# A written order of single operations for the attention part, with the softmax division on ScalarE

## The chip, the core and the metric

The kernel runs on one core of one Trainium2 chip. The core's engines work side by side, each on its own instruction queue in the order in which the queue was written: TensorE multiplies matrices (PE in the profile, PEld for its weight loads), VectorE (DVE) and ScalarE (ACT) work elementwise, GpSimd (POOL) helps in the last part, and SyncE (SP) issues DMA transfers. They hand work to each other through semaphores. The metric is the device time of one execution in microseconds; the median of three runs of the kernel before is 886.98 us (886.62 to 888.88).

## The reference

Three layers follow each other, all in float32. The first is local attention with block summaries, over 2 batches, 8 heads, 768 positions and head dimension 64:

```python
k_sum = k.reshape(B, H, nb, block, D).max(axis=3)        # block 32
v_sum = v.reshape(B, H, nb, block, D).mean(axis=3)
scores_l = where(|i - j| < 16, scale * q @ k.T, -1e9)
scores_s = scale * q @ k_sum.T + log(block)
a = exp(concat(scores_l, scores_s) - max)
a = a / (sum(a) + 1e-9)
x = a @ concat(v, v_sum)                                 # 1536 tokens x 512
```

The second is a PReLU layer, `g = max(h, 0) + alpha * min(h, 0)` with `h = x @ w_in` (512 to 2048), then `g @ w_out`. The third is four experts of width 1024, weighted by normalized probabilities: `out += p[:, e] * (relu(x @ w1[e]) @ w2[e])`. The weights of the second layer arrive as 64-bit words, which the kernel takes apart on the chip.

## The kernel before

**The first part** holds the attention and the first quarter of the PReLU layer, woven into each other. Its order is the table `ORDER`: a list of short names, each of them one step, and the loop at line 625 issues the steps one after the other under a manual schedule. On each engine, and in SyncE's DMA queue, instructions stand in just that order. The first two letters of a name say which step, the digits which piece of the work:

- Attention goes by 24 half-tiles (128 tokens, 4 of the 8 heads). `fa`, `fb` and `fc` load keys, queries and values, `ka` and `va` whole rows of keys and values for the block summaries, `kb` takes the maximum over blocks (line 154) and `vb` the sum (line 164). For half-tile i: `sa` scores on TensorE (line 200), `sb` mask and row maximum on VectorE (line 210), `sc` four exponentials with their row sums on ScalarE (line 219), `na` the division by the sums (lines 224 to 229), `ta` four transposes on TensorE (line 235), `tb` a copy out of PSUM on ScalarE, `xa` probabilities times values on TensorE (line 253), `xb` and `xc` the split of the result into a high and a low half. The tile `sm` of scores, later of probabilities, has three buffers: it is taken by `sb` and given back by `ta`.
- The weights come in pieces of 128 x 512, 16 of them in this part. `wa` loads a piece of 64-bit words (line 282, tile `raw`, three buffers), `wb` cuts out the exponent (line 286), `wc` shifts it on ScalarE (line 291), `wd` builds the fraction (two instructions, lines 296 and 299), `we` the value (three, lines 305 to 309), `wf` the high half on ScalarE (line 314), `wg` the low half (line 320).
- The PReLU layer goes by blocks of 256 tokens. `la` to `le` are a first-layer product of twelve matmuls and its evacuation (the first of them in time is `la01`), `ma` and `mb` a second-layer product and its sum.

**After the table** a scheduler that works from a timeline of its own places the rest of the PReLU layer (matmuls of 512 columns; weight pieces by `w_step`, side by side with the products), and then the 32 expert steps. Both parts run through the same TensorE queue, so the second part begins where the first ends.

Of the kernel before, what the change touches and what calls it, by code (L numbers as in the profile page):

```python
# [8 lines left out]
F32 = mybir.dt.float32  # L9
F32R = mybir.dt.float32r  # L10
U32 = mybir.dt.uint32
AF = mybir.ActivationFunctionType
ALU = mybir.AluOpType
# [4 lines left out]
P = 128  # L18
# [5 lines left out]
NK = KW + NB  # L24
# [22 lines left out]


ORDER = (
# [30 lines left out]
)  # L80
MASK_OFF = -1.0e9 * math.sqrt(D)
EXP_LOW = float((1023 - 127 + 20) << 20)
EXP_TOP = float((255 - 20) << 20)
# [3 lines left out]
def kernel(  # L87
# [15 lines left out]
    nc = tc.nc  # L103
# [10 lines left out]
    att = first.enter_context(tc.tile_pool(name="att", bufs=2))  # L114
# [20 lines left out]
    st = {}  # L135
# [79 lines left out]
    def a_exp(i):  # L215
        sm, mx = st["p", i], st.pop(("m", i))
        st["e", i] = sume = att.tile([P, 4], F32, tag="sume", name="sume", bufs=3)
        for u in range(4):
# [2 lines left out]
                accum_out=sume[:, u:u + 1],  # L221
            )

    def a_norm(i):
        pp, sume = st["p", i], st.pop(("e", i))
        r = att.tile([P, 4, 1], F32, tag="r", name="r")
        nc.vector.tensor_scalar(r[:, :, 0], sume, 1e-9, None, op0=ALU.add)
        nc.vector.reciprocal(r, r)
        nc.vector.tensor_tensor(pp, pp, r.to_broadcast([P, 4, NK]), op=ALU.mult)  # L229

    def a_transpose(i):
        pp = st.pop(("p", i))
# [41 lines left out]
    ws, pw = {}, {}  # L274

    def w_load(p):
        if p >= len(pieces):
            return
        k, i = pieces[p]
        t = wp.tile([P, DM, 2], U32, tag="raw", name="raw", bufs=3)  # L280
        pw[p] = [t]
        return nc.sync.dma_start(out=t.rearrange("p n w -> p (n w)"), in_=wa_in[k, i])

    def w_mask(p):
        e = wp.tile([P, DM], F32, tag="e", name="e")
        nc.vector.tensor_scalar(e.bitcast(U32), pw[p][0][:, :, 1], 0x7FF00000, None, op0=ALU.bitwise_and)
        pw[p].append(e)

    def w_exp(p):
        e = pw[p][1]  # L290
        nc.scalar.activation(e, e.bitcast(U32), AF.Relu, bias=ebias)

    def w_frac(p):
        raw = pw[p][0]
        t = wp.tile([P, DM], F32, tag="t", name="t")
        nc.vector.tensor_scalar(  # L296
            t.bitcast(U32), raw[:, :, 1], 0x000FFFFF, 0x00100000, op0=ALU.bitwise_and, op1=ALU.bitwise_or
        )
        nc.vector.scalar_tensor_tensor(t, raw[:, :, 0], 2.0 ** -32, t.bitcast(U32), op0=ALU.mult, op1=ALU.add)  # L299
        pw[p].append(t)  # L300

    def w_value(p):
        raw, e, t = pw[p]
        eu = e.bitcast(U32)
        nc.vector.tensor_scalar(eu, e, EXP_TOP, 8.0, op0=ALU.min, op1=ALU.mult)  # L305
        nc.vector.scalar_tensor_tensor(  # L306
            eu, raw[:, :, 1], 0x80000000, eu, op0=ALU.bitwise_and, op1=ALU.bitwise_or
        )
        nc.vector.tensor_tensor(t, t, e, op=ALU.mult)  # L309

    def w_high(p):
# [9 lines left out]
        ws[k, i] = ws[k, i], lo  # L321

    def w_step(p):
        for f in (w_mask, w_exp, w_frac, w_value, w_high, w_low):
            f(p)
        w_load(p + 3)

# [278 lines left out]
    def block(f):  # L606
        return lambda u, j: f(j, u * C0, C0)

    def column(f):
# [4 lines left out]
        "va": v_load, "vb": v_sum, "vc": v_rows,  # L614
        "vd": lambda b: v_mean(b, 0), "ve": lambda b: v_mean(b, 1),
        "fa": load_kw, "fb": load_q, "fc": load_vw,
        "sa": a_scores, "sb": a_max, "sc": a_exp, "na": a_norm, "ta": a_transpose, "tb": a_copy,
        "xa": a_pv, "xb": a_xh, "xc": a_xl,
        "wa": w_load, "wb": w_mask, "wc": w_exp, "wd": w_frac, "we": w_value, "wf": w_high, "wg": w_low,
        "la": block(l1_product), "lb": block(l1_minus), "lc": block(l1_prelu), "ld": block(l1_high),  # L620
        "le": block(l1_low), "ma": column(l2a_product), "mb": column(l2a_sum),
    }
# [14 lines left out]
    for p in range(4 * G, 4 * G + 3):  # L637
        w_load(p)
# [9 lines left out]
    for u, (n, c0, size) in enumerate(units):  # L648
        last = u + 1 == len(units)
        main = [lambda j=j: l1_step(u, j) for j in range(1, G)]  # L650
        if not last:
            main.append(lambda: l1_step(u + 1, 0))
        main += l2_steps(u)
        if n < NG1 - 1:
            p0 = (n + 1) * 2 * G
            lo, hi = ((c0 * 2 * G // (B * S)), ((c0 + size) * 2 * G // (B * S)))
            side = [lambda p=p: w_step(p) for p in range(p0 + lo, min(p0 + hi, len(pieces)))]
        elif c0 == 0:
            side = [lambda: e_load_a(0), lambda: e_load_b(0)]
        elif not last:  # L660
            side = e_prep(0)
        else:
            side = sum(x_combine(0, lambda: gp.tile([P, TP], F32, tag="m", name="m", bufs=2)), [])
        merge(main, side)
# [82 lines left out]
```

## Time and profile before

| | |
|---|---|
| median of 3 runs | 886.98 us |
| the profiled execution | 888.12 us, span 886.3 us |
| TensorE (PE) busy | 834.1 us (94%) |
| TensorE weight loads (PEld) | 739.3 us (83%) |
| VectorE (DVE) busy | 561.8 us (63%) |
| ScalarE (ACT) busy | 391.0 us (44%) |
| GpSimd (POOL) busy | 325.3 us (37%) |
| granted TensorE clock, mean | 0.986 |

The span runs from the first to the last instruction. Busy shares are means over a program whose parts have different limits, so the table alone does not say which engine sets the time; windows of time and the order of single instructions do. A line number is that of the kernel before. In a timeline row the first number is the start in us, the second the length; on VectorE and ScalarE an instruction often starts a little before the end of the one in front of it, so what an instruction costs its engine is the distance to the next start.

### The profile page before, as it was taken

How to read it: one execution, taken by the hardware profiler on the slowest of the kernel's cores; microseconds unless marked ns; L12 is line 12 of the kernel's file. 1: busy time of each engine (PE TensorE's matmuls, PEld its weight loads, DVE VectorE, ACT ScalarE, POOL GpSimd, SP SyncE). 2: the span in 40 equal slices, each digit the busy share in tenths (PEclk: the TensorE clock that was granted, in tenths of full speed). 3: DMA queues.
4: the chain of work that ended last, by engine and by line, in shares of the span. 5: the costliest groups of instructions: out<-in, count | busy, mean ns of one | idle time of the engine just before them, and what ended most of it. 6: DMA issues, size and time to landing. Idle time of an engine off the chain costs nothing.

```text
span 886.3 us, 12629 instructions
## 1 busy us (share of the span) xinstructions
PE 834.1 (94%) x4616; PEld 739.3 (83%) x4616; DVE 561.8 (63%) x1167; ACT 391.0 (44%) x891; POOL 325.3 (37%) x326
## 2 busy tenths in 40 slices
PE   2478989999999999999999999999999999999998
PEld 1367888988888888888988999899898999999896
DVE  6998999797786344665554544555855455455544
ACT  3465877553332232463444343444444444344420
POOL 0000000000002230176766667575566666657400
PEclk9789999999999999999999999999999999999999
DMA  9686663131121000021313121121321212112001
GB/s 322 227 242 194 192 181 109 50 118 39 57 72 48 24 24 24 1 72 50 94 48 95 48 90 54 53 91 48 124 91 48 96 47 92 52 63 81 25 1 71
DMA packets 39550, 76.60 MB, mean 86 GB/s; under 512 B 3776, under 2 KB 15296, under 8 KB 39488
## 3 DMA queue, kind: packets, MB, share of 16 engines
q1 hardware_dynamic: 38912, 75.51, 26.7%
q8 instruction: 36, 0.59, 0.3%
q10 hardware_dynamic: 576, 0.28, 0.1%
q14 instruction: 26, 0.21, 0.1%
HBM read 72.63 MB, written 3.15 MB: 85 GB/s over the span
## 4 chain that ended last, share of the span: by engine, by line
PE 82%; DVE 13%; DMA 2%; ACT 1%; issue 1%; ACTq 0%; SPq 0%; DVEq 0%
PE l L394 55%; PE cb L503 15%; PE cd L503 7%; PE ca L503 3%; DVE sm L210 1%; PE s L200 1%; DMA kv<-in_kt 1%; DVE t L299 1%; DVE sm L229 1%; DVE e L306 1%; DVE t L309 1%; DMA vcat<-in_vw 1%; DVE vs L164 1%; DVE e L305 1%; DMA prob_sb<-in_probs 1%
## 5 line engine op out<-in xcount | busy, mean ns | idle before, releaser
L348 POOL TENSOR_TENSOR w0l<-ra,w0h 128x512 fp32r<-128x512 f32 (+1 forms) x64 | 66.2, 1035 | 331.8 <-DVE t L296 263.9
L573 DVE SCALAR_TENSOR_TENSOR acc<-l,prob_sb,acc 128x512 f32<-128x512 f32 x180 | 130.2, 747 | 85.7 <-PE l L394 85.3
L394 PE MATMUL l<-w1h,gh 128*128 128x512 f32 x384 | 150.2, 392 | 1.6 <-ACT gh L519 1.0
L394 PE MATMUL l<-w1l,gh 128*128 128x512 f32 x384 | 150.8, 393 | 0.0
L394 PE MATMUL l<-w1h,gl 128*128 128x512 f32 x384 | 145.3, 394 | 0.0
L348 POOL TENSOR_TENSOR w1l<-rb,w1h 128x512 fp32r<-128x512 f32 x64 | 83.6, 1309 | 120.1 <-ACT w1h L347 120.1
L348 POOL TENSOR_TENSOR w0l<-s,w0h 128x512 fp32r<-128x512 f32 x64 | 83.9, 1311 | 37.3 <-ACT w0h L347 36.8
L394 PE MATMUL l<-xh,w0h 128*128 128x512 f32 (+1 forms) x240 | 85.0, 354 | 3.0 <-DVE gl L426 2.1
L394 PE MATMUL l<-gh,w1h 128*128 128x512 f32 (+1 forms) x240 | 83.8, 352 | 3.0 <-ACT gh L420 2.9
L394 PEld LDWEIGHTS l<-w1h,gl 128*128 128x128 f32 x384 | 71.9, 188 | 15.7 <-DVE gl L520 0.4
L394 PEld LDWEIGHTS l<-w1h,gh 128*128 128x128 f32 x384 | 72.1, 188 | 13.7 <-ACT gh L519 1.4
L394 PE MATMUL l<-gh,w1l 128*128 128x512 f32 (+1 forms) x240 | 83.4, 349 | 0.0
L394 PE MATMUL l<-xl,w0h 128*128 128x512 f32 (+1 forms) x240 | 83.4, 347 | 0.0
L394 PE MATMUL l<-xh,w0l 128*128 128x512 f32 (+1 forms) x240 | 83.2, 347 | 0.0
L394 PE MATMUL l<-gl,w1h 128*128 128x512 f32 (+1 forms) x240 | 81.7, 351 | 1.4 <-DVE gl L426 1.4
L347 ACT ACTIVATE w0h<-s 128x512 fp32r<-128x512 f32 x64 | 40.5, 632 | 94.4 <-PE cd L503 71.8
L394 PEld LDWEIGHTS l<-w1l,gh 128*128 128x128 f32 x384 | 72.1, 188 | 11.0
L347 ACT ACTIVATE w1h<-rb 128x512 fp32r<-128x512 f32 x64 | 40.5, 632 | 77.7 <-PE l L394 56.1
L503 PE MATMUL cb<-xeh,w0h 128*128 128x384 f32 x192 | 64.7, 337 | 0.1
L503 PE MATMUL cb<-xeh,w0l 128*128 128x384 f32 x192 | 64.7, 337 | 0.0
L503 PE MATMUL cb<-xel,w0h 128*128 128x384 f32 x192 | 64.7, 337 | 0.0
L347 ACT ACTIVATE w0h<-ra 128x256 fp32r<-128x256 f32 (+1 forms) x64 | 33.6, 525 | 56.4 <-PE cb L503 36.5
(112 smaller groups left out, 1797.2 us busy)
## 6 DMA issues: line engine op xcount, KB each, us to landing
raw<-in_wa SPq DMA_DIRECT2D x32, 512.0 KB, 4.2
ra<-in_wb SPq DMA_DIRECT2D x64, 256.0 KB, 3.8
rb<-in_wb SPq DMA_DIRECT2D x32, 512.0 KB, 3.6
q<-in_qh SPq DMA_DIRECT2D x24, 256.0 KB, 4.2
kw<-in_kw SPq DMA_DIRECT2D x24, 192.0 KB, 4.7
vcat<-in_vw SPq DMA_DIRECT2D x12, 384.0 KB, 4.4
kv<-in_kt SPq DMA_DIRECT2D x8, 384.0 KB, 4.1
kv<-in_vt SPq DMA_DIRECT2D x8, 384.0 KB, 4.7
```

Of the source, the lines that this page charges most:

```text
L164: nc.vector.tensor_reduce(vs[:, hp, KW:NK], st.pop(("v", b, hp)), axis=AX.X, op=ALU.add)
L200: nc.tensor.matmul(sp[:, u], q[:, u // 2, u % 2], kw[:, :, u // 2, u % 2], start=True, stop=True)
L210: nc.vector.tensor_tensor_reduce(sm[:, u], sp[:, u], mask[:, m], -1.0 / math.sqrt(D), 3.0e38, ALU.add, ALU.min, mx[:, u:u + 1],)
L229: nc.vector.tensor_tensor(pp, pp, r.to_broadcast([P, 4, NK]), op=ALU.mult)
L299: nc.vector.scalar_tensor_tensor(t, raw[:, :, 0], 2.0 ** -32, t.bitcast(U32), op0=ALU.mult, op1=ALU.add)
L305: nc.vector.tensor_scalar(eu, e, EXP_TOP, 8.0, op0=ALU.min, op1=ALU.mult)
L306: nc.vector.scalar_tensor_tensor(eu, raw[:, :, 1], 0x80000000, eu, op0=ALU.bitwise_and, op1=ALU.bitwise_or)
L347: nc.scalar.activation(hi, src, AF.Copy)
L348: nc.gpsimd.tensor_tensor(lo, src, hi.bitcast(F32), op=ALU.subtract)
L394: ins = nc.tensor.matmul(ps, a, c, start=(i == 0), stop=(i == n - 1))
L503: nc.tensor.matmul(ps, l, r, start=(first and i == 0), stop=(i == len(terms) - 1), skip_group_check=True)
L573: nc.vector.scalar_tensor_tensor(acc2[:, t], ps, pe, acc2[:, t], op0=ALU.mult, op1=ALU.add)
```

## The change

Three things change, all in the first part.

1. The division `na` becomes three steps. `na` adds the guard 1e-9 to the sums, `nb` takes the reciprocal, both on VectorE with 128 x 4 elements, and `nc` multiplies the probabilities on ScalarE: four ACTIVATE instructions of 128 x 120 with the reciprocal as a scale per partition, in place of one VectorE multiplication of 128 x 480.
2. The weight steps are cut up: `wd` and `we` are now the two instructions of the fraction, `wf`, `wg` and `wh` the three of the value, `wi` the high half on ScalarE and `wj` the low half. What they compute stays as it was.
3. `ORDER` is written anew, with 694 names in place of 598. All loads, half-tiles, pieces and products are the same; they stand in another order.

```diff
-    "ka00 ka01 fa0 fb0 fc0 wa3 wa1 wa0 fa1 kb00 fb1 fa2 fb2 kb01 va00 fc2 fa3 kc00 va01 sa0 sb0 fb3 "
+    "ka00 fa0 ka01 fb0 kb00 kb01 kc00 fb2 fa2 sa0 sb0 ka03 sc0 sa2 kb03 sb2 wa1 na0 wb1 ka02 fb4 fa1 "
...
+    def a_guard(i):
+        st["r", i] = r = att.tile([P, 4], F32, tag="r", name="r", bufs=3)
+        nc.vector.tensor_scalar(r, st.pop(("e", i)), 1e-9, None, op0=ALU.add)
+
+    def a_recip(i):
+        nc.vector.reciprocal(st["r", i], st["r", i])
+
     def a_norm(i):
-        pp, sume = st["p", i], st.pop(("e", i))
-        r = att.tile([P, 4, 1], F32, tag="r", name="r")
-        nc.vector.tensor_scalar(r[:, :, 0], sume, 1e-9, None, op0=ALU.add)
-        nc.vector.reciprocal(r, r)
-        nc.vector.tensor_tensor(pp, pp, r.to_broadcast([P, 4, NK]), op=ALU.mult)
+        pp, r = st["p", i], st.pop(("r", i))
+        for u in range(4):
+            nc.scalar.activation(pp[:, u], pp[:, u], AF.Copy, scale=r[:, u:u + 1])
...
-        for f in (w_mask, w_exp, w_frac, w_value, w_high, w_low):
+        for f in (w_mask, w_exp, w_mant, w_frac, w_top, w_sign, w_value, w_high, w_low):
```

The next two pieces are VectorE's queue just behind the first half-tile's row maxima. `e` and `t` are the exponent and fraction of a weight piece, `r` the reciprocal sums of a half-tile, `sm` its probabilities; the number tells one buffer from another. Before:

```order
L286 TENSOR_SCALAR e_160<-raw_119 128x512
L296 TENSOR_SCALAR t_162<-raw_119 128x512
L299 SCALAR_TENSOR_TENSOR t_162<-raw_119,t_162 128x512
L227 TENSOR_SCALAR r_166<-sume_155 128x4
L228 RECIPROCAL r_166<-r_166 128x4
L229 TENSOR_TENSOR sm_146<-sm_146,r_166 128x480
L305 TENSOR_SCALAR e_160<-e_160 128x512
L306 SCALAR_TENSOR_TENSOR e_160<-raw_119,e_160 128x512
L309 TENSOR_TENSOR t_162<-t_162,e_160 128x512
L286 TENSOR_SCALAR e_180<-raw_121 128x512
```

Now, in the same place, though behind the maxima of two half-tiles in place of one (the line numbers are the changed kernel's):

```order
L230 TENSOR_SCALAR r_157<-sume_138 128x4
L295 TENSOR_SCALAR e_159<-raw_155 128x512
L305 TENSOR_SCALAR t_167<-raw_155 128x512
L158 TENSOR_REDUCE ksum_95<-kv_161 128x24
L316 TENSOR_SCALAR e_159<-e_159 128x512
L233 RECIPROCAL r_157<-r_157 128x4
L312 SCALAR_TENSOR_TENSOR t_167<-raw_155,t_167 128x512
L320 SCALAR_TENSOR_TENSOR e_159<-raw_155,e_159 128x512
L162 COPY kw10_98<-ksum_95 128x96
L162 COPY kw11_99<-ksum_95 128x96
L326 TENSOR_TENSOR t_167<-t_167,e_159 128x512
L230 TENSOR_SCALAR r_199<-sume_182 128x4
```

The multiplication of `sm` is gone from here, and between an instruction and the one that reads its result there now stands at least one other: the reciprocal, the fraction's second instruction, the sign and the product each have such a neighbour in front of them, where before five of ten rows read what the row above had just written.

The next two pieces are ScalarE's queue at its start. `sm` with `mx` and `sume` are exponentials, `sm` with `r` the new multiplications, `w0h` the high half of a weight piece. Before:

```order
L219 ACTIVATE sm_218,sume_225<-sm_218,mx_219 128x120 x4
L314 ACTIVATE w0h_239<-t_215 128x512
L291 ACTIVATE e_243<-e_243,ebias_87 128x512
L240 ACTIVATE ptb_256<-pt_245 120x512
L291 ACTIVATE e_263<-e_263,ebias_87 128x512
L314 ACTIVATE w1h_275<-t_253 128x512
```

Now:

```order
L223 ACTIVATE sm_130,sume_138<-sm_130,mx_131 128x120 x4
L300 ACTIVATE e_159<-e_159,ebias_87 128x512
L223 ACTIVATE sm_149,sume_182<-sm_149,mx_150 128x120 x4
L238 ACTIVATE sm_130<-sm_130,r_157 128x120 x4
L331 ACTIVATE w0h_203<-t_167 128x512
L300 ACTIVATE e_201<-e_201,ebias_87 128x512
L238 ACTIVATE sm_149<-sm_149,r_199 128x120 x4
```

Each half-tile now stands in ScalarE's queue twice before its transposes, once for the exponentials and once for the multiplications, and the exponentials of the next half-tile stand between the two.

## Rows read from the trace of the kernel before

**Rows 1.** Windows: us, busy time (instructions), TensorE clock, DMA share, GB/s
```profile
0.00:62.00 62.00, 27.37 (x205) 23.61 (x205) 52.14 (x163) 29.98 (x95) 0.74 (x6) 0.84 0.84 270
62.00:181.50 119.50, 108.78 (x1057) 102.97 (x1056) 108.42 (x349) 79.67 (x263) 0.00 (x0) 0.98 0.48 145
88.00:133.00 45.00, 41.16 (x419) 38.72 (x420) 43.77 (x163) 34.92 (x124) 0.00 (x0) 1.00 0.62 188
181.50:370.00 188.50, 188.50 (x833) 156.13 (x832) 120.03 (x207) 67.56 (x115) 23.85 (x24) 1.00 0.14 45
370.00:886.30 516.30, 509.46 (x2527) 456.56 (x2525) 281.17 (x452) 213.84 (x421) 300.71 (x296) 1.00 0.20 66
```
**Rows 2.** Timeline, TensorE: first 256-column product, first of 512 columns
```profile
61.99 0.56 PE L394 MATMUL l<-xh,w0h 128*128 128x256 f32 x1
...
180.95 0.40 PE L394 MATMUL l<-xh,w0h 128*128 128x512 f32 x1
```
**Rows 3.** Waits of VectorE, 10 to 144 us: total, times, longest
```profile
DVE sm L210 <- PE s L200: 2.1, 2, 1.5
```
**Rows 4.** Timeline, VectorE, 106.1 to 111.6 us
```profile
106.10 0.42 DVE L286 TENSOR_SCALAR e<-raw 128x512 uint32<-128x512 uint32 x1
106.43 0.42 DVE L296 TENSOR_SCALAR t<-raw 128x512 uint32<-128x512 uint32 x1
106.89 0.69 DVE L299 SCALAR_TENSOR_TENSOR t<-raw,t 128x512 f32<-128x512 uint32 x1
107.50 0.48 DVE L416 SCALAR_TENSOR_TENSOR l<-m,beta,l 128x256 f32<-128x256 f32 x1
...
108.22 0.16 DVE L227 TENSOR_SCALAR r<-sume 128x4 f32<-128x4 f32 x1
108.42 0.18 DVE L228 RECIPROCAL r<-r 128x4 f32<-128x4 f32 x1
108.63 0.66 DVE L229 TENSOR_TENSOR sm<-sm,r 128x480 f32<-128x480 f32 x1
109.20 0.42 DVE L426 TENSOR_TENSOR gl<-l,gh 128x256 fp32r<-128x256 f32 x1
109.54 0.41 DVE L305 TENSOR_SCALAR e<-e 128x512 uint32<-128x512 f32 x1
109.99 0.69 DVE L306 SCALAR_TENSOR_TENSOR e<-raw,e 128x512 uint32<-128x512 uint32 x1
110.71 0.69 DVE L309 TENSOR_TENSOR t<-t,e 128x512 f32<-128x512 f32 x1
111.32 0.28 DVE L210 CUSTOM_DVE_ANT_0 sm<-s,mask 128x120 f32<-128x120 f32 x1
```
**Rows 5.** Groups of VectorE by line and shape, 0 to 181.5 us: busy, mean ns
```profile
L229 DVE TENSOR_TENSOR sm<-sm,r 128x480 f32<-128x480 f32 x24 | 15.8, 658 | 0.8
L154 DVE TENSOR_REDUCE ksum<-kv 128x24 f32<-128x768 f32 x8 | 7.6, 947 | 6.9 <-DMA kv<-in_kt 6.9
```
**Rows 6.** Timeline, ScalarE: the first exponential and its row sum
```profile
10.20 0.39 ACT L219 ACTIVATE sm<-sm,mx 128x120 f32<-128x120 f32 x1 [6.30 <-DVE mx L210]
10.50 0.19 ACT L219 ACTIVATION_READ_ACCUMULATOR sm<-sm,mx 128x1 f32 x1
```
**Rows 7.** Timeline, VectorE: maxima of the last half-tile, and what follows them
```profile
152.17 0.28 DVE L210 CUSTOM_DVE_ANT_0 sm<-s,mask 128x120 f32<-128x120 f32 x1 [0.42 <-PE pt L235]
...
152.98 0.69 DVE L306 SCALAR_TENSOR_TENSOR e<-raw,e 128x512 uint32<-128x512 uint32 x1
```
**Rows 8.** Timeline, TensorE: the scores of one half-tile
```profile
50.25 1.05 PE L200 MATMUL s<-kw,q 128*128 128x120 f32 x8
```
**Rows 9.** Timeline: first half-tile's first maximum, last half-tile's transposes
```profile
9.88 0.28 DVE L210 CUSTOM_DVE_ANT_0 sm<-s,mask 128x120 f32<-128x120 f32 x1 [1.45 <-PE s L200]
...
157.69 0.65 PE L235 MATMUL pt<-ident,sm 128*120 128x128 f32 x4
```
**Rows 10.** Waits of SyncE's DMA queue, 0 to 62 us
```profile
SPq L282 <- DVE e L306: 9.4, 4, 4.8
```

More of the change, by code (lines that the diff above doesn't have):

```diff
@@ L280, in w_load @@
         t = wp.tile([P, DM, 2], U32, tag="raw", name="raw", bufs=3)
-        pw[p] = [t]
+        pw[p] = [t, None, None]
         return nc.sync.dma_start(out=t.rearrange("p n w -> p (n w)"), in_=wa_in[k, i])
@@ L286, in w_mask @@
         nc.vector.tensor_scalar(e.bitcast(U32), pw[p][0][:, :, 1], 0x7FF00000, None, op0=ALU.bitwise_and)
-        pw[p].append(e)
+        pw[p][1] = e
     def w_exp(p):
@@ L291, in w_exp, with w_mant @@
         nc.scalar.activation(e, e.bitcast(U32), AF.Relu, bias=ebias)
-    def w_frac(p):
+    def w_mant(p):
         raw = pw[p][0]
@@ L298, in w_frac, with w_top, w_sign @@
         )
+        pw[p][2] = t
+    def w_frac(p):
+        raw, t = pw[p][0], pw[p][2]
         nc.vector.scalar_tensor_tensor(t, raw[:, :, 0], 2.0 ** -32, t.bitcast(U32), op0=ALU.mult, op1=ALU.add)
-        pw[p].append(t)
-    def w_value(p):
[L303 to L308, printed above, removed]
+    def w_top(p):
+        e = pw[p][1]
+        nc.vector.tensor_scalar(e.bitcast(U32), e, EXP_TOP, 8.0, op0=ALU.min, op1=ALU.mult)
+    def w_sign(p):
+        eu = pw[p][1].bitcast(U32)
+        nc.vector.scalar_tensor_tensor(
+            eu, pw[p][0][:, :, 1], 0x80000000, eu, op0=ALU.bitwise_and, op1=ALU.bitwise_or
+        )
+    def w_value(p):
+        _, e, t = pw[p]
         nc.vector.tensor_tensor(t, t, e, op=ALU.mult)
@@ L616 @@
         "fa": load_kw, "fb": load_q, "fc": load_vw,
-        "sa": a_scores, "sb": a_max, "sc": a_exp, "na": a_norm, "ta": a_transpose, "tb": a_copy,
+        "sa": a_scores, "sb": a_max, "sc": a_exp, "na": a_guard, "nb": a_recip, "nc": a_norm, "ta": a_transpose, "tb": a_copy,
         "xa": a_pv, "xb": a_xh, "xc": a_xl,
-        "wa": w_load, "wb": w_mask, "wc": w_exp, "wd": w_frac, "we": w_value, "wf": w_high, "wg": w_low,
+        "wa": w_load, "wb": w_mask, "wc": w_exp, "wd": w_mant, "we": w_frac, "wf": w_top,
+        "wg": w_sign, "wh": w_value, "wi": w_high, "wj": w_low,
         "la": block(l1_product), "lb": block(l1_minus), "lc": block(l1_prelu), "ld": block(l1_high),
```

62 rows, old and new, of the table ORDER are left out of this document.

## The prediction

> **What bounds the kernel now.** I read the busy time in windows first, since the page's shares are means over parts with different limits. From 181.5 to 370 us TensorE is busy 188.50 of 188.50 us, and to the end 509.46 of 516.30 [rows 1]: there TensorE is the bound, and the changed steps do not reach it. The boundary lies where matmuls of 256 columns give way to those of 512, at 180.95 us [rows 2]. So the change is worth what it moves that boundary by, less what it disturbs behind it.
>
> In front of the boundary TensorE is idle for 34.6 us of the first 62 and 10.7 us of the 119.5 behind them, and its clock is at 0.84 of full speed in the first stretch [rows 1]. The reader is to see there that the idle time sits early. What TensorE waits for is VectorE: the list of VectorE's own waits from 10 to 144 us has no entry longer in total than 2.1 us [rows 3], and in the window from 88 to 133 us it is busy 43.77 of 45 us [rows 1]. VectorE's queue is thus the first part's clock until about 144 us. From 62 us on TensorE is close behind (91% busy), so VectorE time saved there buys little; time saved before 62 us buys nearly all.
>
> **What VectorE loses and ScalarE gains.** Costs are distances between starts [rows 4]. The multiplication takes 0.57 us (108.63 to 109.20), 24 times [rows 5]: 13.7 us off VectorE. Next, waits on the instruction in front. The exponent cut at 106.10, which its neighbour does not read, lets that neighbour start after 0.33 us; the fraction's first instruction, of the same size, is read by the next and holds it for 0.46; 109.54 to 109.99 is 0.45 again. The two-input form takes 0.61 when nobody waits (106.89 to 107.50) and 0.72 when the next one reads it (109.99 to 110.71). So a read of what was just written costs about 0.12 us. Before, there are three such pairs per weight piece and two per division, 16 x 3 + 24 x 2 = 96; by my count of the new order 13 stay. 83 x 0.12 = 10.0 us. Together 23.7 us of the 160.6 that VectorE is busy before the boundary (52.14 + 108.42, [rows 1]).
>
> The Trainium skill speaks against the second term: "VectorE: DVE Perf Modes", section "The DRAIN you can't avoid", says that the next operation does not start until the pipeline is empty, with a semaphore or without, so that placing dependents apart would save nothing; a later section there, "Two Vector instructions with no wait between them", allows an earlier start. The rows side with the later section: 0.42 us long, but 0.33 apart when independent. What the first rule would make of the time is the third rival.
>
> ScalarE gets 24 x 4 = 96 instructions of 128 x 120. No such multiplication is in the trace. The nearest row is an exponential of the same shape, also with one operand per partition: 0.30 us from its start to that of its row-sum read [rows 6]. The read itself is not needed now. Bounds: not above 0.49 (with the whole 0.19 us read behind it); from below, a quarter of what VectorE needs for all four, 0.57 / 4 = 0.14. I take 0.30, the same shape: 28.8 us, ends 13.7 and 47.0. ScalarE was busy 29.98 + 79.67 = 109.7 us of 181.5; with this 138.5, level with VectorE's 136.9 and TensorE's 136.2 (27.37 + 108.78). ScalarE had idle time for it everywhere, but no engine is left that is far below the others.
>
> **How far the first part gets shorter.** I follow a marker, `la01`, the first first-layer product, at 61.99 us [rows 2], and count what stands ahead of it in VectorE's queue, before and now. Divisions: eight whole ones of 0.98 us (108.22 to 109.20) against ten guards and nine reciprocals; these are 0.20 each when the next one waits, and with the 0.12 taken off about 0.09: 7.8 against 1.7, -6.1 (the ends of the unknown 0.09, zero and 0.20, make this -7.8 and -4.0). Weight pieces: eight exponent cuts and seven pieces of 0.46 + 0.61 + 0.45 + 0.72 + 0.61 and 0.61 for the low half (taken as the product's), 26.9, against seven cuts, six fractions, and five of the rest without the waits (0.33, 0.33 + 0.61, 0.33 + 3 x 0.61), 18.8: -8.1. Against that, three more half-tiles' maxima at 0.81 [rows 7] and three more key maxima at no more than 0.95 [rows 5], +5.3; two low halves of the attention's output fewer, at 0.34 (109.20 to 109.54), -0.7. Sum -9.6 us. It is more than half the division and the waits; the rest is that the order brings attention forward and pushes weight pieces back.
>
> The marker also has more behind it: scores of 11 half-tiles stand ahead of `la01` in place of 9, two times about 1 us of TensorE [rows 8], so 2 us. Behind the marker, the 119.5 us hold 10.7 of TensorE idle. VectorE, which filled 91% of them, loses the other 14 us; ScalarE gains 15 half-tiles x 1.2 = 18 us on top of 79.7, some 83% of a shorter stretch. I take 2 us gained there: the ends are +8 (idle down to under 3) and -6 (a third engine as full as the others adds waits). Sum 9.6 + 2 + 2 = 13.6 us.
>
> Costed at nothing: the second part is placed by the scheduler in a slightly other interleave up to the experts, and the last weight pieces (14 and 15) finish at the end of the table; VectorE's 120.0 busy of 188.5 us hides both, and without that cover a late piece would cost about its own chain on VectorE, 3.5 us. Eight more issue rows do not arise on SyncE: the loads are the same in number.
>
> Span 886.3 - 13.6 = 872.7. The profiled execution took 888.12 us, 1.14 above the median 886.98, so on the median's scale 886.98 - 13.6 = 873.4, forecast 873. The likeliest case's own range is 865 to 879: gains from 22 (9.6 + 2 + 8, with the guard at its lower end) to 8 (9.6 + 2 - 6 with the guard dear).
>
> **Rivals.**
> *Transfers become the bound.* Ahead of `la01` stand loads of 16.8 MB before (counted in the table, sizes by the tiles' shapes), and 62 us at 270 GB/s are 16.7 MB [rows 1]: the queue had delivered just that. Now 15.7 MB stand ahead; at 270 GB/s they take 58 us, so the marker moves 4 us, and with 2 + 0 to 2 behind it the time is 879 to 881. For it: DMA share 0.84 in that stretch. Against: the weight loads stood waiting 9.4 us for VectorE to release buffers [rows 10], so part of the rate was VectorE's doing, and 0.84 leaves a sixth.
>
> *Slower: the path through ScalarE.* A half-tile keeps one of three `sm` buffers from its first maximum to its transposes, now through ScalarE twice. 24 half-tiles through three buffers are eight rounds; from 9.88 to 158.3 us [rows 9] a round may last 18.6 us, and the last half-tile took 6.2 (152.17 to 158.34, [rows 7, 9]). If the multiplications queue so long behind PSUM copies and weight halves that the hold passes 18.6 us, attention ends later than now: at 20 us a round 160 + 9.9 = 170 us, 11.6 later, 899. It decides from 12 us more wait per half-tile. Against it: ScalarE is 60% busy (109.7 of 181.5) and goes to about 82%. The Trainium skill's "ScalarE: Activation LUTs", section "Rules for kernel authors", sends multiplications to VectorE; here ScalarE does need 28.8 us for what cost 13.7.
>
> *The waits stay.* If every VectorE instruction holds its successor as long as a dependent one, divisions ahead of the marker cost 19 x 0.20 = 3.8 (-4.0) and pieces 7 x 0.33 + 6 x 1.07 + 5 x 2.39 = 20.7 (-6.2): -5.6 us, gain 9.6, 877. Rows 4 speak against it.
>
> *No change.* The total load on the three engines hardly falls, only its distribution; if they fill the stretch no better than before, the boundary stays.
>
> **How the numbers follow.** Likeliest 0.56; transfers 0.16; waits stay 0.03; better than 865 0.07; no change 0.08; slower 0.10. The range drops about half of the better case, the slower one and most of no change: 864 to 884. A measurement of this kernel tells 0.3%, 2.7 us, from no change: faster is 0.56 + 0.16 + 0.03 + 0.07 = 0.82, same 0.08, slower 0.10.
>
> **What would show it.** Right: `la01` near 52 us; the 512-column matmuls begin near 167; VectorE busy near 137 us ahead of that; ScalarE's new instructions about 0.30 us apart; the 0.33 spacing behind nearly all exponent and fraction steps; DMA near 300 GB/s ahead of the marker. Wrong: a marker at 58 us with DMA share still 0.84 (transfers); TensorE's transposes waiting for ScalarE's multiplications for tens of microseconds in sum (the path); idle TensorE just behind the boundary for late weight pieces.

## The result, and the profile after

The changed kernel takes 865.79 us (median of 4 runs, 865.16 to 866.77), the kernel before, run beside it, 887.62 us (886.62 to 888.88): a ratio of 0.9754, with a 95% interval of 0.9737 to 0.9771, or 21.8 us less. The forecast of 873 us had the sign right and the size too small; 865.79 lies near the low end of its range (864 to 884). A second measurement of the changed kernel gives 866.40 us and a ratio of 0.9751 (0.9732 to 0.9771). A single execution of all those measured here, of the kernel with dense queries below, took 1382.82 us at a granted clock of 0.561 (the others of that kernel 0.985 to 0.990), and its ratio leaves that execution out.

The profiled span is 864.0 us in place of 886.3. First the two marks on TensorE's timeline, as in [rows 2] (start, length, instruction):

```profile
49.46 0.39 PE L411 MATMUL l<-xh,w0h 128*128 128x256 f32 x1
...
158.53 0.40 PE L411 MATMUL l<-xh,w0h 128*128 128x512 f32 x1
```

The marker moved from 61.99 to 49.46 us (12.5), the boundary from 180.95 to 158.53 (22.4). From the boundary to the end of the span it is 705.5 us, and was 705.4: all of the gain lies in the first part. The windows up to 62 us, from there to the boundary and behind it, to be read against [rows 1]:

```profile
0.00:62.00 62.00, 39.57 (x320) 34.63 (x320) 50.01 (x196) 47.51 (x172) 0.74 (x6) 0.92 0.95 312
62.00:158.90 96.90, 95.24 (x939) 91.31 (x939) 75.50 (x263) 79.52 (x272) 0.00 (x0) 1.00 0.41 132
158.90:348.00 189.10, 189.10 (x836) 156.62 (x835) 132.13 (x236) 72.47 (x124) 23.51 (x24) 1.00 0.16 56
```

The reader is to see three things. In the first 62 us the DMA engines are busy for 0.95 of the time and move 312 GB/s, where it was 0.84 and 270. Behind them TensorE is busy 95.24 of 96.90 us, where 10.7 of 119.5 were idle. And VectorE, which filled 91% of that stretch before, fills 78% now: it has ceased to be level with TensorE. Of the 160.6 us that it was busy ahead of the boundary, 125.5 are left; the page's totals (561.8 and 539.2 us) say that 22.6 are gone for good, and the other 12 now lie behind the boundary, where VectorE is busy 132.13 of 189.10 us and TensorE still 189.10: there they cost nothing.

What TensorE waits for in the first 62 us (total, times, longest), and the SyncE entry that answers [rows 10], a weight load waiting for VectorE:

```profile
PE s L204 <- DVE kw L162: 8.1, 1, 8.1
PE s L204 <- DMA kw<-in_kw: 3.8, 1, 3.8
PE xps L262 <- DMA vcat<-in_vw: 3.0, 2, 1.7
PE s L204 <- DVE r L233: 3.0, 1, 3.0
```
```profile
SPq L291 <- DVE vs L168: 0.5, 1, 0.5
```

The first wait is the start of the kernel; behind it loads of keys and values are named as often as VectorE. The weight loads stand 0.5 us where they stood 9.4. That is a part of SyncE's queue: by the sums of the same list all its loads together wait 14.4 us for VectorE and 6.2 for TensorE, where it was 18.8 and 15.3 (9.5 and 9.0 in the second measurement of the changed kernel). From 62 us to the boundary no wait of TensorE is longer than 0.6 us in sum.

VectorE's queue in the new order, to be read by the distance between starts as [rows 4]:

```profile
12.96 0.17 DVE L230 TENSOR_SCALAR r<-sume 128x4 f32<-128x4 f32 x1
13.03 0.42 DVE L295 TENSOR_SCALAR e<-raw 128x512 uint32<-128x512 uint32 x1
13.36 0.42 DVE L305 TENSOR_SCALAR t<-raw 128x512 uint32<-128x512 uint32 x1
13.70 0.95 DVE L158 TENSOR_REDUCE ksum<-kv 128x24 f32<-128x768 f32 x1
14.56 0.42 DVE L316 TENSOR_SCALAR e<-e 128x512 uint32<-128x512 f32 x1
14.89 0.17 DVE L233 RECIPROCAL r<-r 128x4 f32<-128x4 f32 x1
14.98 0.66 DVE L312 SCALAR_TENSOR_TENSOR t<-raw,t 128x512 f32<-128x512 uint32 x1
```

Guard and reciprocal hold the queue for 0.07 and 0.09 us (0.20 each before), the exponent, the fraction and the top for 0.33 or 0.34. ScalarE's multiplications, the group over the first 170 us (busy, mean ns | idle before) and four of them on the timeline:

```profile
L238 ACT ACTIVATE sm<-sm,r 128x120 f32<-128x120 f32 x96 | 29.9, 390 | 2.6 <-DVE r L233 2.4
```
```profile
100.91 1.25 ACT L238 ACTIVATE sm<-sm,r 128x120 f32<-128x120 f32 x4
102.05 0.37 ACT L468 ACTIVATE acc<-l 128x256 f32<-128x256 f32 x1
```

Four take 1.14 us from start to start, 0.285 each, and they wait for VectorE 2.4 us in all of the first part.

### The profile page after: what moved, and what is told of

Its sections match the earlier page's. It is cut to its first block, busy times and chain, and to the rows that moved or that the text cites. A ratio compares the mean times of both kernels' runs of the same rounds, so it can differ in the third digit from the quotient of the medians.

```text
span 864.0 us, 12725 instructions
## 1 busy us (share of the span) xinstructions
PE 832.9 (96%) x4616; PEld 738.8 (86%) x4616; DVE 539.2 (62%) x1143; ACT 413.1 (48%) x987; POOL 324.0 (37%) x326
## 4 chain that ended last, share of the span: by engine, by line
PE 90%; DVE 5%; DMA 3%; ACT 1%; issue 0%; SPq 0%; ACTq 0%; DVEq 0%
PE l L411 60%; PE cb L520 15%; PE cd L520 8%; PE ca L520 4%; PE s L204 2%; PE xps L262 1%; DMA kv<-in_vt 1%; DMA kw<-in_kw 1%; DMA raw<-in_wa 1%; PE pt L244 1%; DVE xl L481 1%; DMA alpha_sb<-in_alpha 1%; DVE sm L214 0%; DVE ksum L158 0%; DVE acc L590 0%
## 5 line engine op out<-in xcount | busy, mean ns | idle before, releaser
L411 PEld LDWEIGHTS l<-w1h,gh 128*128 128x128 f32 x384 | 72.1, 188 | 13.7 <-ACT gh L536 1.4
```

The source lines that it names most:

```text
L411: ins = nc.tensor.matmul(ps, a, c, start=(i == 0), stop=(i == n - 1))
```

## Experiments: which of the three edits gains

The theory on record was that VectorE's queue is the clock of the first part, so that the multiplication taken off it and the waits between neighbours are more than half of the gain. The rivals: the order itself, and the transfers. The first four kernels take the three edits apart, as far as one at a time can.

**Only the multiplication moved, in the old order.** The three division instructions stay together where they were; the third is ScalarE's.

```diff
-        nc.vector.tensor_tensor(pp, pp, r.to_broadcast([P, 4, NK]), op=ALU.mult)
+        for u in range(4):
+            nc.scalar.activation(pp[:, u], pp[:, u], AF.Copy, scale=r[:, u, 0:1])
```

> The old order, with only the multiplication of the probabilities moved to ScalarE (four instructions in the place of the one on VectorE). Theory (VectorE's queue sets the first part until about 144 us): VectorE loses 24 x 0.57 = 13.7 us and 24 x 0.12 = 2.9 us of waits, nearly all of it on the path, so the boundary to the 512-column matmuls comes 12 to 16 us earlier, 872 to 876 us. Rival (the written order is what gains; in the old one the multiplications wait in ScalarE's queue behind work placed there for another purpose, and TensorE follows close behind VectorE): at most 5 us, 882 to 888 us.

Measured: 902.28 us beside 889.23, ratio 1.0145 (1.0129 to 1.0160): 13 us slower, outside both expectations. Marker 64.8, boundary 194.4. What TensorE waits for up to 185 us, and then what ScalarE waits for:

```profile
PE pt L236 <- ACT sm L230: 16.1, 6, 7.6
PE s L200 <- DVE kw L158: 11.3, 2, 7.9
PE xps L254 <- ACT ptb L241: 9.4, 8, 2.8
```
```profile
ACT sm L230 <- DVE r L228: 10.9, 10, 3.3
```

The lists fit one reading: a multiplication that stands directly behind its exponentials waits for VectorE's reciprocal (10.9 us in sum), what stands behind it in ScalarE's queue starts later, and TensorE waits for probabilities (16.1) and PSUM copies (9.4). This is the prediction's slower rival, in the old order.

**The new order with the multiplication left on VectorE.** The step `nc` becomes one VectorE instruction.

```diff
-        for u in range(4):
-            nc.scalar.activation(pp[:, u], pp[:, u], AF.Copy, scale=r[:, u:u + 1])
+        nc.vector.tensor_tensor(pp, pp, r.to_broadcast([P, 4, NK]), op=ALU.mult)
```

> The changed kernel with its new order, but the multiplication as one VectorE instruction of 128 x 480, in the place where the four on ScalarE stood. Theory: the changed kernel is bound by loads ahead of its marker and by TensorE behind it, so of VectorE's 24 x 0.57 = 13.7 us only what falls ahead of the marker shows, nine half-tiles, 5 us, and up to 4 more: 871 to 875 us. Rival (ScalarE's multiplication is the whole gain, the order none): 880 us or more. Second rival (the order is all): 865 to 868 us.

Measured: 867.98 us, ratio 0.9761 (0.9741 to 0.9781). Marker 52.4, boundary 161.2. That is the second rival's time: the order is all. Nearly the whole gain is there with 13.7 us more on VectorE; the difference to the full change, 0.0007 of the ratio, is inside the intervals (by the boundaries, 2.7 us). The windows ahead of the boundary:

```profile
0.00:62.00 62.00, 36.98 (x307) 32.10 (x308) 53.71 (x201) 35.14 (x125) 0.74 (x6) 0.83 0.94 304
62.00:161.20 99.20, 96.47 (x952) 92.50 (x951) 84.54 (x281) 67.08 (x223) 0.00 (x0) 1.00 0.42 133
```

The loads run at 304 GB/s and TensorE idles 2.7 us behind 62, close to the full change (312 and 1.7): both come with the order.

**The new order with dependents put back together.** By count 72 instructions of VectorE stand directly behind the one whose result they read, in place of 14; the sequence of the steps is otherwise the new one.

```diff
-    "ka00 fa0 ka01 fb0 kb00 kb01 kc00 fb2 fa2 sa0 sb0 ka03 sc0 sa2 kb03 sb2 wa1 na0 wb1 ka02 fb4 fa1 "
+    "ka00 fa0 ka01 fb0 kb00 kb01 kc00 fb2 fa2 sa0 sb0 ka03 sc0 sa2 kb03 sb2 wa1 wb1 ka02 fb4 fa1 fa4 wc1 "
```

> The changed kernel with its new order, but dependent VectorE instructions put next to each other again where that was possible: fraction's first right ahead of its second, the three of the value in a row, guard right ahead of reciprocal; 72 such pairs in place of 14. Theory: 58 x 0.12 = 7 us more on VectorE, about a third of it ahead of the marker and on the path, the rest in VectorE's idle time: 867.5 to 870 us, and the spacing of such pairs back at 0.45 and 0.72 us. Rival (the waits were never on the path): 865 to 866.5 us. Second rival (VectorE still sets the time everywhere): 872 to 874 us.

Measured: 868.72 us, ratio 0.9767 (0.9747 to 0.9788), boundary 161.9. The spacing is back at 0.45 and 0.73 us, and VectorE is busy 130.5 us ahead of the boundary in place of 125.5:

```profile
16.15 0.42 DVE L315 TENSOR_SCALAR e<-e 128x512 uint32<-128x512 f32 x1
16.60 0.69 DVE L319 SCALAR_TENSOR_TENSOR e<-raw,e 128x512 uint32<-128x512 uint32 x1
17.33 0.69 DVE L325 TENSOR_TENSOR t<-t,e 128x512 f32<-128x512 f32 x1
```

The time is as expected, some 3 us above the full change by the boundary, but the intervals overlap.

**The old order with dependents apart.** The steps are cut up as in the change, the multiplication stays on VectorE, and each instruction that reads its neighbour's result is put a few places later: 9 pairs are left of 96.

> The old order with VectorE's multiplication, only with the weight steps and the division cut up and, where a dependent instruction followed its producer on VectorE, one of the next independent ones pulled in between: 9 such pairs left of 96. Theory (VectorE sets the first part, each wait costs 0.12 us): 87 x 0.12 = 10.4 us off VectorE, the boundary 7 to 10 us earlier, 878 to 881 us. Rival (TensorE follows close behind and keeps most of it): 883 to 887 us.

Measured: 889.44 beside 889.23 us, ratio 1.0004 (0.9995 to 1.0014): nothing, where the theory wanted 8 to 11 us. Marker 60.5, boundary 181.9. The window up to 144 us, in the kernel before and then here, and VectorE's longest waits from 10 to 144 us, where [rows 3] had nothing above 2.1:

```profile
0.00:144.00 144.00, 100.49 (x928) 92.27 (x928) 130.20 (x431) 86.95 (x294) 0.74 (x6) 0.92 0.71 222
0.00:144.00 144.00, 98.90 (x928) 91.21 (x928) 125.05 (x433) 85.75 (x295) 0.74 (x6) 0.99 0.70 222
```
```profile
DVE r L229 <- ACT sm L222: 3.6, 6, 0.8
DVE sm L213 <- PE s L203: 2.7, 3, 1.5
DVE vs L167 <- DMA kv<-in_vt: 1.5, 2, 1.0
```

VectorE is busy 5 us less and waits about as much more, for ScalarE, TensorE and loads. The two rows also speak against TensorE's clock as a cause of the gain: it is 0.99 here where it was 0.92, and the time is the same.

## Experiments: what bounds the first part

**The old order with no multiplication at all.** The one test of the step "VectorE's queue is the clock" that adds nothing elsewhere; the attention's output is left without its division.

```diff
         nc.vector.reciprocal(r, r)
-        nc.vector.tensor_tensor(pp, pp, r.to_broadcast([P, 4, NK]), op=ALU.mult)
```

> The kernel before with the multiplication of the probabilities by the reciprocal sums left out altogether (guard and reciprocal stay; the attention's output is therefore not normalised): 24 x 0.57 us = 13.7 us less on VectorE, with no instruction added on any engine and the order as before. The prediction's step (VectorE's queue is the first part's clock, what it saves there is gained): marker 4 to 5 us earlier, boundary 171 to 175 us, 876 to 881 us beside a kernel before of 889. Rival (the order sets when each engine may start; a saved VectorE microsecond turns into a wait for TensorE or ScalarE, as in old_order_dependents_apart): marker within 2 us of 62, boundary 178 to 181, 885 to 889 us.

Measured: 881.46 us, ratio 0.9920 (0.9897 to 0.9944), between the two expectations: 7 of the 13.7 us. Marker 61.4, boundary 174.0. The windows:

```profile
0.00:62.00 62.00, 30.82 (x207) 25.75 (x208) 47.66 (x157) 30.36 (x96) 0.73 (x6) 0.95 0.85 272
62.00:174.00 112.00, 106.86 (x1051) 101.98 (x1051) 97.58 (x330) 77.79 (x261) 0.00 (x0) 0.98 0.49 154
```

Ahead of the marker VectorE has 4.5 us less to do and the marker moves 0.6 us; the loads run at 272 GB/s with a share of 0.85, as before. What TensorE waits for up to the marker, in the kernel before (one line) and then here (two):

```profile
PE pt L235 <- DVE sm L229: 11.4, 3, 8.6
```
```profile
PE pt L234 <- ACT sm L219: 4.6, 2, 3.7
PE s L200 <- DMA q<-in_qh: 4.4, 1, 4.4
```

The longest entry of before, 11.4 us for the multiplication, is gone, and other waits, for ScalarE and a load, have come in its place: the engine named in a wait was the last to arrive, not the one that sets the marker. Behind it 6.3 us are gained, and TensorE's idle time falls from 10.7 to 5.1 us. Sixteen of the 24 multiplications, 9.1 us, stood behind the marker. So VectorE held TensorE there, for 6.3 us of the 9.1, and ahead of the marker hardly at all. Between this kernel (ratio 0.9920) and the one with the same multiplications on ScalarE (1.0145) lie some 20 us: that is what ScalarE's path costs in the old order. In the new one it costs nothing that can be seen.

**Extra loads in the changed kernel.** Four loads of 0.46 MB that nobody reads stand ahead of the marker.

```diff
+    def extra(i):
+        nc.sync.dma_start(out=junk, in_=wb_in[0, 8 + 2 * i:10 + 2 * i, :, 0:448].rearrange("i p n -> p i n"))
```

> The changed kernel with four extra loads of 128 x 896 words (0.46 MB each, 1.8 MB together) into a tile that nothing reads, in SyncE's queue ahead of the loads of the second, fourth, sixth and seventh further queries, all ahead of the marker. Theory (ahead of the marker the changed kernel waits for transfers, at 312 GB/s): 1.8 MB / 312 GB/s = 5.9 us, marker and boundary 4 to 6 us later, 870 to 872 us. Rival (VectorE's queue sets the marker as before and the transfers run in its shadow): under 1.5 us, 865 to 867 us.

Measured: 870.98 us, ratio 0.9792 (0.9766 to 0.9818). Marker 55.5 and boundary 163.9, 6.0 and 5.3 us later (3.9 and 5.6 beside the second measurement of the changed kernel). The 1.84 MB take 5.9 us at 312 GB/s, and by the boundary nearly that is what they cost. By the ratios it is 3.4 us, and there the intervals just overlap (0.9766 and 0.9771). The first window shows it at a share of 0.98, with VectorE less busy than in the change, and TensorE's wait for key loads is 8.9 us in place of 3.8:

```profile
0.00:62.00 62.00, 36.73 (x270) 32.88 (x271) 46.06 (x178) 43.91 (x155) 0.73 (x6) 0.75 0.98 314
```
```profile
PE s L203 <- DMA kw<-in_kw: 8.9, 3, 4.1
```

The extra loads write the same tile and so wait for each other in SyncE's queue (2.9 us in sum); at a share of 0.98 hardly any transfer time is lost by that.

**Half the query bytes, first try.** The query tiles are half zeros; here only the other half is loaded, into tiles kept zeroed. To keep the rows of a transfer long, the four operands of a half-tile are interleaved, so that TensorE loads its weights with a step of four elements.

```diff
-            nc.tensor.matmul(sp[:, u], q[:, u // 2, u % 2], kw[:, :, u // 2, u % 2], start=True, stop=True)
+            nc.tensor.matmul(sp[:, u], q[:, :, u], kw[:, :, u // 2, u % 2], start=True, stop=True)
```

> The changed kernel without the zeros in the query loads: each half-tile's queries are loaded as two blocks of 64 partitions x 256 words (128 KB in place of 256 KB) into one of three fixed tiles whose other half was set to zero once; the weight load of the scores reads them with a stride of four words. Theory (transfers bound the stretch ahead of the marker): 12 query loads x 0.131 MB = 1.6 MB less ahead of the marker, 5 us at 312 GB/s, of which VectorE's queue keeps some: marker 2 to 5 us earlier, 861 to 864 us. Rival (VectorE's queue bounds it): 865 to 867 us; slower, up to 872, if the strided weight loads or 24 more issues cost more.

Measured: 877.81 us, ratio 0.9871 (0.9846 to 0.9895), slower than the change and outside what was expected. The weight loads of the scores over the first 170 us (busy, mean ns), here and then in the changed kernel:

```profile
L211 PEld LDWEIGHTS s<-kw,q 128*128 128x128 f32 x192 | 46.4, 327 | 16.5 <-issue 14.0 <-DVE t L312 0.7 <-DMA q<-in_qh 0.6
```
```profile
L204 PEld LDWEIGHTS s<-kw,q 128*128 128x128 f32 x192 | 29.1, 234 | 17.8 <-DVE kw L162 8.9 <-issue 4.4 <-DVE e L316 3.2
```

The eight matmul records of a half-tile (two for each of its four products) take 2.01 us in place of 1.04, 23 us over 24 half-tiles. That hides whatever the bytes were worth, so the run says nothing on transfers.

**Half the query bytes, dense operands.** The operands are not padded; each product becomes two, of half the rows and half the columns of the array.

```diff
-            nc.tensor.matmul(sp[:, u], q[:, u // 2, u % 2], kw[:, :, u // 2, u % 2], start=True, stop=True)
+            for j in range(2):
+                r = slice(j * D, (j + 1) * D)
+                nc.tensor.matmul(sp[r, u], q[r, u], kw[r, :, u // 2, u % 2], start=True, stop=True)
```

> The changed kernel with its query tiles loaded without their zero half (128 KB each in place of 256), the stationary operands staying dense: each half-tile's scores are 8 products of 64 x 64 x 120 in place of 4 of 128 x 128 x 120 with zeros. If transfers bound the stretch ahead of the marker, some 1.5 MB less at 312 GB/s is up to 4.9 us: marker 45 to 47, 861 to 864 us. Rival: the rows of a transfer become 1 KB, and the rate falls as in half_queries (277 GB/s from 31 to 62 us): 14.2 MB at 277 GB/s are 51 us, marker 49 to 51, 865 to 868 us. Second rival: twice as many score products cost TensorE more than 0.1 us each behind the marker, where it is full: 24 half-tiles x 4 x 0.1 = 9.6 us at most, 868 to 875 us.

Measured: 864.47 us, ratio 0.9719 (0.9706 to 0.9732); the span is 861.0 us in place of 864.0, the marker at 47.5 and the boundary at 155.5, between the theory's ranges and the first rival's. The first window and the score products (over 170 us):

```profile
0.00:62.00 62.00, 40.80 (x459) 33.63 (x460) 53.37 (x214) 49.78 (x180) 0.74 (x6) 0.86 0.89 286
```
```profile
L206 PE MATMUL s<-kw,q 64*64 64x120 f32 x384 | 29.3, 305 | 14.1 <-DVE kw L162 9.0 <-DVE r L235 3.2 <-DMA q<-in_qh 1.2
```

Twice as many products are busy 29.3 us (32.1 in the changed kernel), so the second rival falls. The gain is 3 us of a possible 4.9, which fits a rate of 286 GB/s in place of 312.

**More work on ScalarE.** Two copies of 128 x 120 that nobody reads follow each half-tile's multiplications, 48 in all, 12.0 us of busy time in the trace.

```diff
+        for u in range(2):
+            nc.scalar.activation(junk[:, u], mask[:, u], AF.Copy)
```

> The changed kernel with two more ScalarE copies of 128 x 120 behind each half-tile's multiplications (from the mask into a tile that nothing reads): 48 x 0.29 = 14 us more on ScalarE, as if its multiplication cost half as much again. Theory (behind the marker TensorE is the bound, ahead of it transfers, and ScalarE has room): under 2 us, 865 to 868 us. Rival (ScalarE is the new bound that the change has made): 6 us or more, 872 to 880 us.

Measured: 866.41 us, ratio 0.9743 (0.9721 to 0.9765), boundary 158.8, as the theory had it. ScalarE has the room.

**The two halves of the order, each alone.** Up to the marker the new order and then the old one with dependents apart, and the reverse. Some names had to be put off until what they read is there (8 and 9 stand later than in the order that they come from), and 24 and 14 names of the second half stand ahead of `la01`.

> The multiplication is one VectorE instruction, as in new_order_dve_mult (867.98 us, marker 52.4, boundary 161.2). The names stand in the new order up to `la01`; behind it in the old order with dependents apart, each put off only as far as its operands ask. Theory (what stands ahead of the marker is what gains: the loads run at full rate there and attention's scores are brought forward, and behind it any order that keeps TensorE fed will do): marker 52 to 53, TensorE idle under 4 us between marker and boundary, boundary 161 to 164, 868 to 871 us. Rival (the order behind the marker has a part of its own): marker 52 to 53, but TensorE idle by some 10 us behind it as before, boundary 169 to 173, 876 to 880 us.

> The reverse of new_order_ahead_only: the old order with dependents apart up to `la01` (marker 60.5 in old_order_dependents_apart), the new order behind it, the multiplication on VectorE. Theory (the gain is made ahead of the marker): marker 60 to 62, boundary 177 to 182, 884 to 889 us. Rival (the order behind the marker removes TensorE's idle time of about 10 us there, whatever stands ahead): marker 60 to 62, boundary 169 to 173, 876 to 880 us.

Measured: 892.98 us, ratio 1.0045 (1.0029 to 1.0062), marker 55.1, boundary 185.3; and 894.48, ratio 1.0064 (1.0042 to 1.0085), marker 66.6, boundary 188.2. Both are slower than before and outside all four expectations. The waits lie at the seam, where one order takes over from the other. In the first the scores of the twelfth half-tile start at 54.2 us and of the thirteenth at 91.2, since the old order brings its attention later. In the second, TensorE has one wait above 2 us between 55 and 98 us, and from 75 to 92 us it is busy 5.72 of 17 us:

```profile
PE xps L260 <- ACT xh L273: 13.8, 1, 13.8
```
```profile
75.00:92.00 17.00, 5.72 (x38) 5.63 (x39) 8.05 (x26) 4.18 (x16) 0.00 (x0) 0.52 0.52 176
92.00:186.00 94.00, 92.15 (x914) 88.36 (x914) 75.77 (x258) 61.33 (x208) 0.00 (x0) 1.00 0.37 112
```

The last row shows that beyond the seam the new order keeps TensorE busy 92.15 of 94 us. The old order in the first kernel has 87.81 there:

```profile
92.00:186.00 94.00, 87.81 (x857) 83.43 (x857) 80.22 (x268) 63.26 (x207) 0.00 (x0) 0.98 0.40 125
```

That fits an order that gains behind the marker too, but a spliced order is not one of its halves, and the share of each stays open.

**The changed kernel once more.**

> The changed kernel itself once more, in more rounds, for the comparison with dense_queries (ratio 0.9719, 0.9706 to 0.9732, beside 0.9754, 0.9737 to 0.9771, of its first measurement). If the dense queries are worth the 3 us that their spans say (861.0 and 864.0 us): ratio 0.974 to 0.977. Rival (the first measurement was of another chip, and they are worth nothing): 0.971 to 0.973.

Measured: 866.40 us, ratio 0.9751 (0.9732 to 0.9771), marker 51.6, boundary 158.3. Against it the dense queries are 0.0032 lower, some 2.8 us; the intervals just meet at 0.9732, and the two ran on different chips. They are the better version by all that was measured, though their lead over the change is no larger than its uncertainty. The two executions also show how far a mark is to be trusted: the boundary agrees within 0.2 us, the marker differs by 2.2.

## Why the prediction came out as it did

**What held.** The second part did not move (705.5 us behind the boundary). The sizes on the engines were right: VectorE loses 22.6 us (forecast 23.7), the spacing behind a neighbour that is not read is 0.33 us, ScalarE's multiplications stand 0.285 us apart (0.30). The DMA rate near 300 GB/s came, at 312. The marker was forecast near 52 and stood at 49.5 and 51.6, for another reason than the forecast's. The boundary, forecast near 167, stood at 158.5. The waits-stay rival falls with the 0.33 rows. "No change" falls with the result.

**The step that failed: "VectorE's queue is thus the first part's clock until about 144 us".** It was read from the absence of long waits on VectorE, and that a queue hardly ever waits does not make it what the others wait for. Taking 13.7 us off it moved the marker by 0.6 us and the boundary by 7; spreading the dependents moved nothing. The marker came out near 52 by luck: it was a sum of VectorE terms, and they do not act there. The kernel with the division on VectorE has its marker at 52.4, level with the second execution of the full change. "Time saved before 62 us buys nearly all", and behind it little, was the wrong way round: in the old order VectorE's time counted behind the marker.

**What stands in its place ahead of the marker: loads.** They bound the changed kernel there, as the extra loads show (the boundary 5.3 us later for 1.84 MB). For the kernel before it is an inference: by the prediction's own count 16.8 MB stood ahead and 15.7 stand there now; at 270 GB/s the difference is 4 us, and 15.7 MB at 312 in place of 270 GB/s are 7.8 us less, together 11.9 beside the 12.5 measured (10.4 by the second execution). By this inference the transfers rival had the right resource and the wrong price, since it kept the rate at 270. Why the rate rose is not shown. The prediction had a part of a reason in hand and gave it as an argument against: the weight loads stood 9.4 us for buffers that VectorE held [rows 10], and stand 0.5 now. All of SyncE's waits for VectorE and TensorE fell by 13.5 us (15.6 in the second execution), in part for each of the two engines; no run takes out one of them alone.

**The mis-sized term: 2 us behind the marker, ends +8 and -6.** From marker to boundary it was 118.96 us and is 109.07 (106.7 in the second execution): 10 to 12 us less. The term for two more half-tiles' scores ahead of the marker, 2 us, is part of this, so the remaining 8 to 10 are to be set beside the 2, at or just above its upper end of +8. Between the same two marks TensorE's idle time fell from 10.7 to 3.7 us (1.9 in the second execution), 7 to 9 us, and its work by about 3. The lower end, that three engines equally full would hinder each other, did not come, though they were about as full as forecast: VectorE 125.5 and ScalarE 127.0 us of 158.9 (79 and 80%; forecast 136.9 and 138.5 of 167, 82 and 83%). The 12 us of VectorE's work that now lie behind the boundary are weight pieces of the second part: 16 fractions are built ahead of it, where there were 20.

**The range.** Two of its ends do not follow from the prediction's own terms. With the guard at its lower end (1.7 us more), 9.6 + 2 + 8 makes a gain of 21.3 us and not 22; with the guard dear (2.1 us less), 9.6 + 2 - 6 makes 3.5 and not 8. The likeliest case thus reached from 866 to 883 us in place of 865 to 879. The measured gain of 21.8 lies just above the upper end of that case; inside the stated range it fell with the marker right by luck and the stretch behind it sized too small.

**The slower rival.** A path through ScalarE was priced for the new order at 899 us and given 0.10. It came true in the old order (902.28). What differs is the place of the multiplications: behind the exponentials of another half-tile, as the new ScalarE queue has them, they wait 2.4 us; directly behind their own, 10.9. That this place decides is argued from the waits; no run moves it alone.

**Where the 21.8 us come from.** The new order with the multiplication on VectorE, and dependents still apart, gives 21 (ratio 0.9761). ScalarE's multiplication and the separation, each taken out alone, are worth about 3 us by the boundary (161.2 and 161.9 without them, 158.5 with), which the times don't tell from nothing; in the old order the one costs 13 us and the other is worth nothing. No run has the new order without both, so up to some 6 of the 22 us may be theirs together. What in the order brings the rest is split only by place, 10 to 12.5 us ahead of the marker and 10 to 12 behind it.

## What to carry to other kernels

A queue that never waits is not yet the bound: take work off it without adding any elsewhere and see whether the end moves, before more than half of a forecast is hung on it. The engine that a wait names is no proof either: here an 11.4 us wait went away with its cause, and the marker moved by 0.6. Where several engines pass small pieces to each other, the written order decides what a faster instruction is worth; the same move of a multiplication was worth at most 3 us in one order and cost 13 in the other. And a resource's rate in the trace of before (270 GB/s here) is a result of the order as well, not a constant to divide bytes by; look at what the loads stood waiting for.

## What the runs showed of the hardware

A float32 weight load of 128 x 128 whose elements stand four apart took 327 ns on average, a dense one 234; a group of eight matmul records behind such loads took 2.01 us in place of 1.04. Score products of 64 x 64, two for one of 128 x 128, took no more TensorE time in all than the padded ones (29.3 and 32.1 us of busy time for 384 and 192 records). With query rows of 1 KB in place of 2 the loads of the first 62 us ran at 286 GB/s (dense) and 273 (first try), with a DMA share of 0.89 and 0.93, where the changed kernel had 312 at 0.95; no run changes the row length alone.
